# Layer 1 reads three of its four blocks from the buffers in which layer 0 left them

## The chip, the cores and the metric

The kernel runs on one core of a Trainium2 chip. That core has a tensor engine for matrix products (PE; its weight loads are shown as PEld), a vector engine (DVE), a scalar engine (ACT), GpSimd (POOL) and SyncE (SP), which here issues most of the transfers between the memory outside the core (DRAM) and the on-chip memory (SBUF). PE writes into a small second memory, PSUM, from which DVE and ACT read. Each engine runs its own list of instructions in order and waits at the head of it. The metric is the device time of one execution in microseconds (us).

## What is computed

Two layers over an input x of 2048 rows and 512 columns (f32). Each layer is a long convolution over the rows, one kernel of 2048 taps per column, and then a gated FFN with a hidden size of 1376. Both get a normalised x and add their result to x:

```
x = x + A(layernorm(x))      # y = causal convolution over the rows, + u * Dskip
x = x + B(layernorm(x))      # (silu(x @ w_gate) * (x @ w_up)) @ w_down
x = x + A(layernorm(x))      # layer 1: the same weights
x = x + B(layernorm(x))
```

## The kernel before

The rows are cut into four blocks of 512. A pair (layer, block) is a unit of work, and `SEQ` (line 43) lists the eight pairs in the order in which they are written: (0,0), (0,1), (0,2), (1,0), (0,3), (1,1), (1,2), (1,3). The convolution of a block works on spectra of 1024 points, in two halves h of 256 columns and four parts q. Block b multiplies the spectra of its own and of all b earlier blocks with those of the taps.

The steps of one unit, by name and line:

- `inputs` (713) loads the block's x into the tile `n` (`load_x`, 234), normalises it in place (`norm_x`, 252: ACT sums the rows into a scrap tile `junk` at 223 and 225, POOL and DVE make the factors at 227 and 228, ACT writes `n` at 255), and `forward` (259) transforms it: ACT and DVE split `n` into two f16 parts `z` (267, 268), PE multiplies at 277 into the PSUM tiles `pf`, ACT and DVE add and subtract into `fu` and `fbt` (278 to 293). POOL stores the spectra to DRAM (`udr`, 739). There is one buffer for `n`.
- `ssm_half` (749) loads earlier spectra `uu` and those of the taps `w` (808, 810), multiplies and adds on DVE (812, 815, 820, 821: seven of the instructions at 812 and 815 for each of the four parts of a half of block 3), and transforms back: ACT and DVE split into `yl` (776, 777), PE multiplies at 784 into the PSUM tiles `pi`, DVE adds `pi` to x in the block's buffer `xt` (`result`, 787; recorded at line 232). Before that, `load_x` at 830 brings x into `xt`.
- `pf` and `pi` take turns in two small PSUM buffers.
- `ffn_norm` (874) normalises `xt` once more, transposes it through DMA, and `ffn` (915) multiplies: `pgu` (930 to 933, two PSUM buffers), ACT and DVE make `sg`, `hh` and `hl` (936 to 939), `py` (946 to 948). At line 953 DVE adds `py` to `xt`. This is the unit's result. For layer 1 it is stored to `out` (955), for layer 0 to a DRAM tensor `xdr` with a place for every block (957).

There are three buffers for `xt`: `xs[0]` and `xs[1]` are halves of the tile `xg`, `xs[2]` is the tile `xf`. A unit takes buffer number (its place in `SEQ`) modulo 3: 0, 1, 2, 0, 1, 2, 0, 1. In layer 1 a unit loads its x from `xdr` twice, once into `n` and once into `xt`.

The loop at line 1263 writes, for each i, the convolution of unit i + 1 and then the FFN of unit i. `inputs` runs one part ahead: the first part of unit i + 2, with load and norm, is written with the last part of unit i + 1, so ahead of the FFN of unit i. Within this stage a planner puts each engine's instructions in order: from times that it reckons in advance, it takes the ready one of highest priority. The instructions in `tc.high_priority` (the products at 277 and 784, the FFN's norm, `sg`, `hh`, `hl` and the residual) go ahead of the others. All that comes before, up to about 330 us, is ordered by hand and isn't touched by the change.

Of the kernel before, what the change touches and what calls it, by code (L numbers as in the profile page):

```python
# [11 lines left out]
F32 = mybir.dt.float32  # L12
F16 = mybir.dt.float16
BF16 = mybir.dt.bfloat16
I32 = mybir.dt.int32
AF = mybir.ActivationFunctionType
# [5 lines left out]
L, D, F = 2048, 512, 1376  # L22
P = 128
T = 512
NB = L // T
# [15 lines left out]
INV = 2  # L41
LOW = [a for a in range(1, 33) if a % 2] + [8, 16, 24, 32]
SEQ = ((0, 0), (0, 1), (0, 2), (1, 0), (0, 3), (1, 1), (1, 2), (1, 3))


def dft_constants():
# [29 lines left out]
def kernel(ctx, tc, x, a_re, a_im, b_re, b_im, c_re, c_im, log_dt, d_skip,  # L76
                           w_gate, w_up, w_down, c_ef, c_ei, c_ek, c_am, c_eh, c_eih, out):
    nc = tc.nc
# [10 lines left out]
    def tl(shape, name, tag, dt=F32):  # L89
        return sb.tile(shape, dt, name=name, tag=tag, bufs=BUFS[tag])  # L90
# [59 lines left out]

    wdr = dram.tile([NB, 2, 4, P, NQ, 2, DC], F32, name="wdr")
    udr = [dram.tile([NB - 1, 2, 4, P, NQ, 2, DC], F32, name=f"udr{i}") for i in range(NL)]
    xdr = dram.tile([NB, 4, P, D], F32, name="xdr")
    kdr = dram.tile([2, 4, 32, 4, 256], F32, name="kdr")
    ndr = dram.tile([2, 2, P, 2, HD], F32, name="ndr")

# [74 lines left out]
    def stt(o, i0, s, i1, op1):  # L231
        V.scalar_tensor_tensor(o, i0, s, i1, OP.mult, op1)  # L232

    def load_x(xt, layer, b):
        if layer == 0:
            nc.sync.dma_start(xt, x[0, b * T:(b + 1) * T, :].rearrange("(p c) d -> p c d", p=P))
        else:
            nc.sync.dma_start(xt, xdr[b].rearrange("c p d -> p c d"))

    def parted(t):  # L240

# [7 lines left out]

        return t.rearrange("p i (c d) -> p i c d", c=NQ)  # L250

    def norm_x(n):
        rs, nb = row_stats(n, 4, 1.0, "stats", lambda r: tl([P, D], "junk", "t1", BF16))
        for c in range(4):
            A.activation(n[:, c], n[:, c], AF.Identity, scale=rs[:, c:c + 1], bias=nb[:, c:c + 1])

    fs, fss = [], []

# [454 lines left out]
    def inputs():  # L713

        for layer, b in SEQ:
            if layer == 0 and b < 2:
                if b == 0:
                    nc.sync.dma_start(u4, udr[0][0, 0].rearrange("q p c i d -> p q c i d"))
                for h in range(2):
                    for i, q in enumerate(QORD):  # L720
                        if b == 0:
                            u = u4[:, q]
                            for qn in (QORD[:3], QORD[3:], (), ())[i] if h else ():
                                nc.sync.dma_start(u4[:, qn], udr[0][0, 1, qn])
                        else:
                            u = tl([P, NQ, 2, DC], "u", "u")
                            nc.sync.dma_start(u, udr[0][b, h, q])
                        yield h, q, u
                continue
            n = tl([P, 4, D], "n", "n")  # L730
            load_x(n, layer, b)
            norm_x(n)
            if (layer, b) == SEQ[HALF]:
                eh.append(tl([P, 4, 2, 2, P], "eh", "ef", F16))
                nc.sync.dma_start(eh[0], c_eh)
            for h in range(2):
                for q, u in forward(n, h, eh[0]):
                    if b < NB - 1:
                        G.dma_start(udr[layer][b, h, q], spectrum(u))
                    yield h, q, u  # L740
# [8 lines left out]
    def ssm_half(layer, b, h):  # L749
        first = layer == 0 and b == 0  # L750
        half = SEQ.index((layer, b)) >= INV
        hs = slice(h * HD, (h + 1) * HD)
        free = iv[h] if first else iv[0]

        def slot():
            return free.pop(0) if free else tl([P, 2, HD], "yf", "w")

        def done(t):
            if any(t is o for o in ivs):
                free.append(t)  # L760
        if half and not yl2:
            yl2.append(tl([P, 2, 2, 2, HD], "yl2", "hf", F16))

        def add_sub(x, y):

            t = slot()
            V.tensor_tensor(t, x, y, OP.add)
            V.tensor_tensor(x, x, y, OP.subtract)
            done(y)
            return t, x  # L770

        def inverse(pi, r, v):

            if half:
                yl = yl2[0][:, r % 2]
                A.activation(yl[:, 0], v, AF.Copy, scale=sy[:, 0:1])
                stt(yl[:, 1], v, sy[:, 0:1], yl[:, 0], OP.subtract)
            with tc.high_priority(offset=0 if first else BOOST):
                if half:
                    terms = [(eih[:, r, i, le], yl[:, ly, i]) for i in range(2) for le, ly in ((0, 0), (0, 1), (1, 0))]  # L780
                else:
                    terms = [(ei[:, r, i], v[:, i]) for i in range(2)]
                for k, (e, o) in enumerate(terms):
                    PE.matmul(pi[:, r % 2], lhsT=e, rhs=o, start=k == 0, stop=k == len(terms) - 1)  # L784
            done(v)

        def result(pi, r):

            o = xt[:, r:r + 2, hs]
            if half:  # L790
                stt(o, pi, sy[:, 1:2], o, OP.add)
            else:
                V.tensor_tensor(o, o, pi, OP.add)

        xt = xs[SEQ.index((layer, b)) % 3]
        ys = []
        for s in range(4):
            hq, q, u = ahead.pop(0)
            nxt = next(spec, None)
            if nxt:  # L800
                ahead.append(nxt)
            yk = tl([P, NQ, 2, 2, DC], "yk", "y1")
            for k in range(b + 1):
                if k == 0:
                    w, uu = w0r[:, h, q], spectrum(u) if any(u is o for o in fss) else u
                else:
                    w = tl([P, NQ, 2, DC], "w", "w")
                    nc.sync.dma_start(w, wdr[k, h, q])
                    uu = tl([P, NQ, 2, DC], "uu", "uu")
                    nc.sync.dma_start(uu, udr[layer][b - k, h, q])  # L810
                t = tl([P, NQ, 2, 2, DC], "t", "t") if k else yk
                V.tensor_tensor(t, uu.unsqueeze(2).to_broadcast([P, NQ, 2, 2, DC]),  # L812
                                w.unsqueeze(3).to_broadcast([P, NQ, 2, 2, DC]), OP.mult)
                if k:
                    V.tensor_tensor(yk, yk, t, OP.add)  # L815
            if any(u is o for o in fss):
                fs.append(u)
            y = slot()
            yo = whole(y)
            V.tensor_tensor(yo[:, 0], yk[:, :, 0, 0], yk[:, :, 1, 1], OP.subtract)  # L820
            V.tensor_tensor(yo[:, 1], yk[:, :, 0, 1], yk[:, :, 1, 0], OP.add)
            if (layer, b, h, s) == (0, 1, 0, 0):
                yield
            ys.append(y)
            if s % 2:
                ys[s - 1:] = add_sub(*ys[s - 1:])
            if s == 3:
                a_, b_, c_, d_ = ys
                if h == 0 and not first:
                    load_x(xt, layer, b)  # L830
                pi = psml([P, 2, HD], "pi")
                v0 = slot()
                V.tensor_tensor(v0, a_, c_, OP.add)
                inverse(pi, 0, v0)
                v1 = slot()
                V.tensor_tensor(v1[:, 0], b_[:, 0], d_[:, 1], OP.subtract)
                V.tensor_tensor(v1[:, 1], b_[:, 1], d_[:, 0], OP.add)
                inverse(pi, 1, v1)
            yield
        pj = psml([P, 2, HD], "pi")  # L840
        V.tensor_tensor(a_, a_, c_, OP.subtract)
        done(c_)
        inverse(pj, 2, a_)
        V.tensor_tensor(b_[:, 0], b_[:, 0], d_[:, 1], OP.add)
        V.tensor_tensor(b_[:, 1], b_[:, 1], d_[:, 0], OP.subtract)
        done(d_)
        inverse(pj, 3, b_)
        result(pi, 0)
        yield
        result(pj, 2)  # L850
        yield
# [22 lines left out]
    def ffn_norm(layer, b, s):  # L874

        rows = TB // P
        xt = xs[SEQ.index((layer, b)) % 3][:, s * rows:(s + 1) * rows]
        nh, nlo = nhl2[:, s % 2, 0], nhl2[:, s % 2, 1]
        with tc.high_priority(offset=BOOST):
            rs, nb = row_stats(xt, rows, 256.0, "stats2", lambda r: nn2[:, r])  # L880
# [34 lines left out]
    def ffn(layer, b, ready=None):  # L915
        for s in range(T // TB):
            rows = TB // P
            xt = xs[SEQ.index((layer, b)) % 3][:, s * rows:(s + 1) * rows]
            nh, nlo = ready if ready and s == 0 else ffn_norm(layer, b, s)
            for f0 in (0, 2, 4, 6, FT - 1, 8) if ready and s == 0 else (FT - 1, 0, 2, 4, 6, 8):  # L920
                pgu = pbig([P, 2, 2, TB], "pgu")
# [21 lines left out]
            for r, f in steps if final else sorted(steps, key=lambda o: o[1]):  # L943
                rc = slice(r * P, (r + 1) * P)
                n = min(P, F - f * P)
# [6 lines left out]
                with tc.high_priority(offset=BOOST):  # L952
                    V.scalar_tensor_tensor(xt[:, r], py[r], sc6[:, 5:6], xt[:, r], OP.mult, OP.add)
                    if layer == NL - 1:
                        nc.sync.dma_start(out[0, b * T:(b + 1) * T, :].rearrange("(p c) d -> c p d", c=4)[c], xt[:, r])
                    else:
                        nc.sync.dma_start(xdr[b, c], xt[:, r])

    ts = [None] * (NCH + 2)
    gs = [None] * (NCH + 2)  # L960
# [346 lines left out]
```

## Time and profile before

| what | us |
|---|---|
| median of 3 runs (lowest to highest) | 1092.52 (1089.46 to 1093.47) |
| the profiled execution | 1091.58 |
| its span, first to last instruction | 1089.4 |
| PE busy / DVE busy / ACT busy | 1026.5 / 969.3 / 547.4 |
| mean granted clock of PE | 0.986 |

How the rows are read. A row of the timeline has the start in us from the span's start, the duration in us, the engine, the line, the operation, output <- inputs by the names of the program, shapes, a count, and in brackets how long the engine had stood idle and what ended that. A row of the waits has who waited, for whom, the total in us, how often, and the longest. A row of the stages has the window, its length, and for each engine the busy time and the number of instructions, then the granted clock, the share of time that the DMA engines worked, and GB/s. A row of the transfers has out<-in, the queue, the count, the KB of one and the median us from issue to landing. `xg` and `xf` stand for the buffers `xs`, `in_A_u_dram` for the input x.

### The profile page before, as it was taken

To read this page: it belongs to the slowest core of one execution; us is meant where nothing else is said; L and a number is where in the kernel's file an instruction comes from. 1 tells how busy PE (TensorE), PEld (TensorE's weight loads), DVE (VectorE), ACT (ScalarE), POOL (GpSimd) and SP (SyncE) were. 2 spreads that over 40 slices of the span, in tenths; PEclk is the share of its full clock that TensorE was granted. 3 is DMA by queue.
4 is the path that set the end of the run, shared out by engine and by line. 5 is a ranking of instruction groups with operands and counts; after the bars stand their busy time and mean duration, and the time that the engine had idled before them with its cause. 6 is when DMAs were issued, how large, how long until landed. Compare 5 with 4: busy or idle time off the path is not lost.

```text
span 1089.4 us, 22811 instructions
## 1 busy us (share of the span) xinstructions
PE 1026.5 (94%) x9302; PEld 810.9 (74%) x9302; DVE 969.3 (89%) x1405; ACT 547.4 (50%) x1093; POOL 109.6 (10%) x163
## 2 busy tenths in 40 slices
PE   1989999998779999999999999999999999999998
PEld 1868888887677777686779676786867687686775
DVE  8999999998999999999999989999998999993221
ACT  6989998953367162466462253533425432134211
POOL 1112222220002010012010001201100000000000
PEclk9989999998989999999999999999999999999999
DMA  5366777768765356342444553443545245312000
GB/s 212 108 180 167 173 166 179 187 181 272 234 182 172 120 145 215 105 141 68 131 117 133 158 160 130 119 136 100 166 126 180 59 127 147 109 61 63 2 25 20
DMA packets 125003, 149.23 MB, mean 137 GB/s; under 512 B 50897, under 2 KB 75985, under 8 KB 124130
## 3 DMA queue, kind: packets, MB, share of 16 engines
q1 hardware_dynamic: 112994, 122.27, 36.8%
q0 software_dynamic: 11904, 25.50, 10.0%
q8 instruction: 73, 1.20, 0.5%
q14 instruction: 32, 0.26, 0.1%
HBM read 97.66 MB, written 33.82 MB: 121 GB/s over the span
## 4 chain that ended last, share of the span: by engine, by line
PE 27%; DVE 27%; issue 11%; DMA 5%; ACT 3%; POOL 1%; SPq 0%; DVEq 0%; POOLq 0%; ACTq 0%
PE pgu L930 5%; PE pgu L931 5%; PE pgu L933 5%; DVE t L812 4%; DVE yk L815 4%; PE py L948 3%; PE py L946 3%; PE py L947 3%; DVE yk L812 3%; PE pi L784 2%; DVE sg L937 2%; DVE hl L939 2%; DMA n<-xdr 1%; DVE yl L232 1%; DMA mix<-nn 1%
## 5 line engine op out<-in xcount | busy, mean ns | idle before, releaser
L930 PE MATMUL pgu<-mix,wsl 128*128 128x256 f16 x1280 | 298.6, 273 | 5.4 <-DVE sg L937 2.1
L931 PE MATMUL pgu<-mix,wsl 128*128 128x256 f16 x1280 | 298.4, 273 | 0.0
L933 PE MATMUL pgu<-mix,wsl 128*128 128x256 f16 x1280 | 194.8, 273 | 0.0
L931 PEld LDWEIGHTS <-wsl 128*128 128x128 f16 x1280 | 125.2, 98 | 22.5 <-issue 6.7
L933 PEld LDWEIGHTS <-wsl 128*128 128x128 f16 x1280 | 125.2, 98 | 18.4 <-issue 3.8
L930 PEld LDWEIGHTS <-wsl 128*128 128x128 f16 x1280 | 125.2, 98 | 16.4 <-issue 1.2
L946 PE MATMUL py<-wsl,hh 128*128 128x512 f16 (+1 forms) x352 | 134.2, 381 | 0.1
L948 PE MATMUL py<-wsl,hl 128*128 128x512 f16 (+1 forms) x352 | 133.5, 381 | 0.1
L947 PE MATMUL py<-wsl,hh 128*128 128x512 f16 x320 | 121.8, 381 | 0.0
L815 DVE TENSOR_TENSOR yk<-yk,t 128x1024 f32<-128x1024 f32 x96 | 116.9, 1218 | 0.5
L812 DVE TENSOR_TENSOR t<-uu,w 128x1024 f32<-128x1024 f32 x96 | 117.0, 1218 | 0.3
L938 ACT ACTIVATE hh<-sg 128x512 f16<-128x512 f32 x80 | 50.1, 627 | 114.0 <-DVE sg L937 114.0
L544 PE MATMUL pw<-kt,ek 128*128 128x256 f32 (+1 forms) x384 | 93.2, 381 | 0.0
L937 DVE SCALAR_TENSOR_TENSOR sg<-pgu,sc,sg 128x512 f32<-128x512 f32 x80 | 59.6, 745 | 37.7 <-ACT sg L936 37.6
L936 ACT ACTIVATE sg<-pgu,sc 128x512 f32<-128x512 f32 x80 | 54.2, 678 | 70.7 <-PE pgu L933 66.9
L544 PEld LDWEIGHTS pw<-kt,ek 128*128 128x128 f32 x384 | 74.8, 199 | 8.8
L939 DVE TENSOR_TENSOR hl<-sg,hh 128x512 f16<-128x512 f32 x80 | 54.8, 685 | 15.3 <-ACT hh L938 15.3
L227 POOL TENSOR_TENSOR rs<-mv,mhalf 128x2 f32<-128x2 f32 (+1 forms) x21 | 33.6, 1598 | 336.3 <-ACT mv L226 296.3
L509 PE MATMUL pk<-re,g 128*32 128x64 f32 x1024 | 65.0, 317 | 2.2 <-DMA g<-g 1.9
L948 PEld LDWEIGHTS <-hl 128*128 128x128 f16 (+1 forms) x352 | 34.4, 98 | 39.2 <-issue 0.8
L947 PEld LDWEIGHTS <-hh 128*128 128x128 f16 (+1 forms) x352 | 34.6, 98 | 38.4 <-issue 0.8
L510 PE MATMUL pk<-im,g 128*32 128x64 f32 x1024 | 63.1, 301 | 0.0
(265 smaller groups left out, 2010.1 us busy)
## 6 DMA issues: line engine op xcount, KB each, us to landing
uu<-udr SPq DMA_DIRECT2D x96, 256.0 KB, 3.0
w<-wdr SPq DMA_DIRECT2D x96, 256.0 KB, 2.8
g<-g POOLq DMA_DIRECT2D x6, 1024.0 KB, 9.2
udr<-fu POOLq DMA_DIRECT2D x22, 256.0 KB, 2.7
udr<-u SPq DMA_DIRECT2D x16, 256.0 KB, 3.3
n<-xdr SPq DMA_DIRECT2D x4, 1024.0 KB, 6.4
kdr<-ks SPq DMA_DIRECT2D x6, 512.0 KB, 2.9
kt<-kdr SPq DMA_DIRECT2D x24, 128.0 KB, 3.0
```

Of the source, the lines that this page charges most:

```text
L509: PE.matmul(o, lhsT=g[:, 0, :, d], rhs=re[:, 0:64, d], start=True, stop=False, tile_position=(0, 32 * grp))
L544: PE.matmul(pw[:, i], lhsT=e, rhs=kt[:, :, c + 4 * k0:4 * k1:4, :].rearrange("p g k d -> p k g d"), start=c == 0, stop=c == 3)
L812: V.tensor_tensor(t, uu.unsqueeze(2).to_broadcast([P, NQ, 2, 2, DC]), w.unsqueeze(3).to_broadcast([P, NQ, 2, 2, DC]), OP.mult)
L815: V.tensor_tensor(yk, yk, t, OP.add)
L930: PE.matmul(o, lhsT=wgu(wi, k, 0)[:, fs], rhs=nh[:, k], start=k == 0, stop=False)
L931: PE.matmul(o, lhsT=wgu(wi, k, 1)[:, fs], rhs=nh[:, k], start=False, stop=False)
L933: PE.matmul(o, lhsT=wgu(wi, k, 0)[:, fs], rhs=nlo[:, k], start=False, stop=k == 3)
L937: V.scalar_tensor_tensor(sg, pgu[:, 1], sc6[:, 4:5], sg, OP.mult, OP.mult)
L939: V.tensor_tensor(hl[:, f0:f0 + 2], sg, hh[:, f0:f0 + 2], OP.subtract)
L946: PE.matmul(py[r], lhsT=hh[:n, f, rc], rhs=wd(f, 0)[:n], start=f == 0, stop=False)
L947: PE.matmul(py[r], lhsT=hh[:n, f, rc], rhs=wd(f, 1)[:n], start=False, stop=False)
L948: PE.matmul(py[r], lhsT=hl[:n, f, rc], rhs=wd(f, 0)[:n], start=False, stop=f == FT - 1)
```

## The change

The buffers are given out by a table, `HOME`, in place of the count modulo 3. Blocks 0, 1 and 3 have the same buffer in both layers (0, 1 and 2); block 2 has buffer 2 in layer 0 and buffer 0 in layer 1. Between the layers only block 2 goes through `xdr`, which shrinks to one block. For the other three, `norm_x` in layer 1 reads the block's buffer and writes `n`, and the convolution's result is added where x already lies.

```diff
+HOME = (0, 1, 2, 0, 2, 1, 0, 2)
+MOVED = 2
...
-    xdr = dram.tile([NB, 4, P, D], F32, name="xdr")
+    xdr = dram.tile([4, P, D], F32, name="xdr")
...
+    def moved(layer, b):
+        return layer == 0 or b == MOVED
+
...
-            nc.sync.dma_start(xt, xdr[b].rearrange("c p d -> p c d"))
+            nc.sync.dma_start(xt, xdr.rearrange("c p d -> p c d"))
...
-    def norm_x(n):
-        rs, nb = row_stats(n, 4, 1.0, "stats", lambda r: tl([P, D], "junk", "t1", BF16))
+    def norm_x(n, xt):
+        rs, nb = row_stats(xt, 4, 1.0, "stats", lambda r: tl([P, D], "junk", "t1", BF16))
         for c in range(4):
-            A.activation(n[:, c], n[:, c], AF.Identity, scale=rs[:, c:c + 1], bias=nb[:, c:c + 1])
+            A.activation(n[:, c], xt[:, c], AF.Identity, scale=rs[:, c:c + 1], bias=nb[:, c:c + 1])
...
             n = tl([P, 4, D], "n", "n")
-            load_x(n, layer, b)
-            norm_x(n)
+            xt = n if moved(layer, b) else xs[HOME[SEQ.index((layer, b))]]
+            if xt is n:
+                load_x(n, layer, b)
+            norm_x(n, xt)
...
-        xt = xs[SEQ.index((layer, b)) % 3]
+        xt = xs[HOME[SEQ.index((layer, b))]]
...
-                if h == 0 and not first:
+                if h == 0 and not first and moved(layer, b):
                     load_x(xt, layer, b)
...
-                    else:
-                        nc.sync.dma_start(xdr[b, c], xt[:, r])
+                    elif moved(1, b):
+                        nc.sync.dma_start(xdr[c], xt[:, r])
```

`ffn_norm` and `ffn` take their buffer from `HOME` in the same way. The unit (0,3) thereby has buffer 2 instead of buffer 1, so its x is loaded into the buffer that the unit (0,2) leaves.

More of the change, by code (lines that the diff above doesn't have):

```diff
@@ L876, in ffn_norm @@
         rows = TB // P
-        xt = xs[SEQ.index((layer, b)) % 3][:, s * rows:(s + 1) * rows]
+        xt = xs[HOME[SEQ.index((layer, b))]][:, s * rows:(s + 1) * rows]
         nh, nlo = nhl2[:, s % 2, 0], nhl2[:, s % 2, 1]
@@ L917, in ffn @@
             rows = TB // P
-            xt = xs[SEQ.index((layer, b)) % 3][:, s * rows:(s + 1) * rows]
+            xt = xs[HOME[SEQ.index((layer, b))]][:, s * rows:(s + 1) * rows]
             nh, nlo = ready if ready and s == 0 else ffn_norm(layer, b, s)
```

## The prediction

> **What bounds the kernel now.** I read the page first: the busy times of the engines.
>
> ```profile
> span 1089.4 us, 22811 instructions
> PE 1026.5 (94%) x9302; PEld 810.9 (74%) x9302; DVE 969.3 (89%) x1405; ACT 547.4 (50%) x1093; POOL 109.6 (10%) x163
> ```
>
> Two engines look full, so an average decides nothing. Next the view of stages. From 390 us on the kernel does what the change touches: the blocks after the first ones, conv of one block beside the FFN of another.
>
> ```profile
> core 0: us, PE busy (x) PEld busy (x) DVE busy (x) ACT busy (x) POOL busy (x), PEclk, DMA share, GB/s
> 390.00:920.00 530.00, 517.51 (x4314) 392.90 (x4312) 510.18 (x756) 230.87 (x451) 40.97 (x55) 1.00 0.45 133
> 920.00:1000.00 80.00, 80.00 (x636) 59.36 (x634) 63.65 (x89) 29.72 (x54) 1.80 (x4) 1.00 0.25 72
> 1000.00:1089.00 89.00, 85.20 (x710) 63.87 (x707) 20.91 (x31) 14.74 (x24) 0.20 (x1) 1.00 0.08 25
> ```
>
> Up to 920 us both PE (517.51 of 530) and DVE (510.18) are full. In the last 169 us DVE works 63.65 + 20.91 = 84.56 us and PE 165.2. So conv is done early and PE carries on alone at a granted clock of 1.00: the end is set by PE's work plus the time PE stands still. The matmuls aren't changed. What can be won is PE's idle time, which is 12.49 us before 920. The view of waits, PE alone, from 390 us on, says for whom it stood:
>
> ```profile
> PE pi L784 <- ACT yl L776: 5.8, 4, 2.0
> PE pf L277 <- ACT fbt L278: 2.5, 1, 2.5
> PE pgu L930 <- DVE sg L937: 2.1, 2, 1.6
> PE pf L277 <- ACT z L267: 1.0, 1, 1.0
> PE pi L784 <- DVE yl L232: 0.3, 1, 0.3
> ```
>
> That is 11.7 us in nine waits, the ceiling of any gain: 1091.58 - 11.7 = 1079.9 us. Six of the nine end with ACT, although ACT is only 230.87 of 530 us busy. ACT isn't slow, it is held: its queue runs in order.
>
> **What the change removes.** Loads and stores of x between the layers:
>
> ```profile
> n<-xdr SPq DMA_DIRECT2D x4, 1024.0 KB, 6.4
> xg<-xdr SPq DMA_DIRECT2D x3, 1024.0 KB, 8.0
> xf<-xdr SPq DMA_DIRECT2D x1, 1024.0 KB, 5.6
> xdr<-xg SPq DMA_DIRECT2D x12, 256.0 KB, 3.9
> ```
>
> Of these (and of four more stores, xdr<-xf) only block 2's remain: three loads into n, three into xs and 12 stores go, 9 MB. With DMA at a share of 0.45, the bytes themselves are worth nothing: no wait of PE above names a transfer.
>
> The loads into xs lie hidden too: DVE's adds at line 789 need them, and no wait names them. They go for nothing.
>
> The loads into n are not hidden. In the timeline, ACT's first instruction on a loaded n is the head of ACT's queue, and what stands behind it is late. ACT first, then the PE rows that follow:
>
> ```profile
> 433.08 0.63 ACT L223 ACTIVATE junk<-n 128x512 bf16<-128x512 f32 x1 [2.74 <-DMA n<-xdr]
> 536.14 0.63 ACT L223 ACTIVATE junk<-n 128x512 bf16<-128x512 f32 x1 [3.51 <-DMA n<-xdr]
> 638.30 0.63 ACT L223 ACTIVATE junk<-n 128x512 bf16<-128x512 f32 x1 [4.55 <-DMA n<-xdr]
> 825.03 0.63 ACT L223 ACTIVATE junk<-n 128x512 bf16<-128x512 f32 x1 [5.30 <-DMA n<-xdr]
> ...
> 436.30 0.27 PE L784 MATMUL pi<-yl,mix 128*128 128x256 f16 x1 [1.41 <-ACT yl L776]
> 539.33 0.27 PE L784 MATMUL pi<-yl,mix 128*128 128x256 f16 x1 [2.02 <-ACT yl L776]
> 633.14 0.27 PE L930 MATMUL pgu<-mix,wsl 128*128 128x256 f16 x1 [1.64 <-DVE sg L937]
> 837.63 0.38 PE L277 MATMUL pf<-z,eh 128*128 128x256 f16 x2 [0.99 <-ACT z L267]
> ```
>
> The four ACT rows are blocks 0, 1, 2 and 3 of layer 1. Block 2 keeps its load. For block 1, say: ACT stands from 532.6 to 536.14, runs its norm, and yl gets its turn only then; PE idles 2.02 us for it. The three loads that go account for 1.41 + 2.02 + 0.99 = **4.42 us** of PE's idle time.
>
> When will the data be there instead? When the FFN's residual (line 953) has written it:
>
> ```profile
> 418.67 0.75 DVE L953 SCALAR_TENSOR_TENSOR xg<-py,sc,xg 128x512 f32<-128x512 f32 x1
> 520.29 1.40 DVE L953 SCALAR_TENSOR_TENSOR xg<-py,sc,xg 128x512 f32<-128x512 f32 x2
> 813.65 0.74 DVE L953 SCALAR_TENSOR_TENSOR xg<-py,sc,xg 128x512 f32<-128x512 f32 x1
> ```
>
> Those end at 419.42, 521.69 and 814.39, so the norm may begin 13.7, 14.5 and 10.6 us earlier than it does. ACT's instructions are the same in number and shape, so they cost what they cost; the last four, which write n, still wait until n's former reader is done. What is late next is PSUM and DVE: pf shares two small buffers with pi, so an early norm doesn't bring pf forward by as much. I therefore count the PE waits named, and no more.
>
> SyncE also stands at the head of its own queue for the stores:
>
> ```profile
> SPq L238 <- DMA xdr<-xg: 4.1, 1, 4.1
> SPq L238 <- DMA xdr<-xf: 2.1, 1, 2.1
> ```
>
> The first (block 3) goes. The second (block 1's load into xs, at 620.76 below) goes, but a load for block 3 of layer 0 stands there instead with the same wait. Behind them are loads of w and uu, which no DVE wait names: nothing.
>
> **What it adds.** Block 3 of layer 0 moves from the buffer of block 1 to that of block 2, whose FFN ends just before. Its load and its first adds now, beside that FFN's end:
>
> ```profile
> 524.02 0.33 SPq L236 DMA_DIRECT2D xg<-in_A_u_dram  x1
> ...
> 612.64 0.74 DVE L232 SCALAR_TENSOR_TENSOR xg<-pi,sy,xg 128x512 f32<-128x512 f32 x1
> 616.90 1.40 DVE L953 SCALAR_TENSOR_TENSOR xf<-py,sc,xf 128x512 f32<-128x512 f32 x2
> 619.35 0.75 DVE L232 SCALAR_TENSOR_TENSOR xg<-pi,sy,xg 128x512 f32<-128x512 f32 x1
> 620.76 0.37 SPq L238 DMA_DIRECT2D xf<-xdr  x1
> ```
>
> Before, the load is issued 88 us ahead of its use. After, it needs the residual of block 2 (ends 618.30) and the store of it. That is the condition of the xf<-xdr load at 620.76, and it lands 5.6 us later, at 626.4. So the adds of block 3's first half, now at 612.64 and 619.35, can't run before 626.4. Their place in DVE's queue is at the earliest behind the residual that they depend on, at 618.3, so DVE can stand 626.4 - 618.3 = 8.1 us at most for this landing. Behind it in the queue would be block 3's products of the second half, sg and hl of the FFN, and so PE's next pgu.
>
> The trace has no such wait on DVE, so I bound it. How much other work is at hand there, the stage says, and how long the products behind it are, the group of line 812:
>
> ```profile
> 612.00:627.00 15.00, 15.00 (x156) 12.33 (x154) 14.97 (x20) 3.25 (x6) 0.00 (x0) 1.00 0.63 215
> ```
> ```profile
> L812 DVE TENSOR_TENSOR t<-uu,w 128x1024 f32<-128x1024 f32 x96 | 117.0, 1218 | 0.3
> ```
>
> Of DVE's 14.97 us the two adds are 1.5 and the residual 1.4, so 12 us are other work. The cost is nothing if the order puts that first; a gain I exclude, as the load starts 97 us later than now. Its other end is 8.1 us, and 628.8 - 618.3 = 10.5 us if the landing takes the 8.0 us of xg<-xdr. The nearest row is block 2's wait: a load of the same 1 MB at the same place, 4.55 us on ACT and **1.64 us** on PE. I take that. The two PSUM buffers of pi are held some 7 to 14 us longer as well; pf of the next block follows later. But ahead of that block's products stand those of block 3's second half, four parts of seven such instructions, 4 x 7 x 1.218 = 34 us, so I count nothing.
>
> **Sum**, against the profiled execution's own time of 1091.58 us (span 1089.4 and 2.2 around it; 0.9 below the median of 1092.52): 1091.58 - 4.42 + 1.64 = **1088.8 us**.
>
> **Rivals.**
>
> *The reused buffer holds DVE (slower).* Place: the add into xs[2] right behind line 953, near 618 us. Price: up to 10.5 us of DVE, which PE feels as soon as both pgu buffers wait for sg. It decides if the products aren't put ahead of the add. For it: DVE is full up to 920, so nothing is caught up there; the orders before are optimistic about loads, as all four ACT rows show. Against: the 12 us of other work at hand. Uncovered, and the three waits of PE back in the shifted order behind it: 1091.58 + 8.1 = 1099.7. With those gains kept: 1087.16 + 8.1 = 1095.3, and 1097.7 with the longer landing.
>
> The Trainium skill (Trainium Kernel Development and Optimization, section Best Practices) advises double-buffering so that DMA overlaps with compute, and here a rotation of three is given up at one place. By that rule the sum is this rival's. The load at 524.02, 88 us ahead of its use, is what the rule asks for, and the trace agrees that no add waited for it.
>
> *Nothing changes (1091.6).* PE's waits come from the order in which pi and pf are put ahead of pgu, not from the loads, and return elsewhere when the order is made anew. For it, PE waits with none of these loads just ahead of them, in PE's timeline:
>
> ```profile
> 476.53 0.27 PE L784 MATMUL pi<-yl,mix 128*128 128x256 f16 x1 [0.99 <-ACT yl L776]
> 665.30 0.27 PE L784 MATMUL pi<-yl,mix 128*128 128x256 f16 x1 [1.40 <-ACT yl L776]
> 868.32 0.81 PE L277 MATMUL pf<-z,eh 128*128 128x256 f16 x6 [2.50 <-ACT fbt L278]
> ```
>
> Against: three waits follow directly on the loads that go.
>
> *The earlier norms cure more (faster).* Ten to 14 us of slack ahead of pf and of block 3's conv take away all PE waits but block 2's (1.64) and the one of 0.99: 11.7 - 2.6 = 9.1, so 1082.5. For it: the 2.50 us on fbt fall in block 3's forward transform, 43 us behind its late norm at 825.03. Against: pf waits for PSUM.
>
> **Chances.** Forecast, 1085 to 1091: 0.36, of which 0.06 lies beyond 0.5% (5.5 us, about what a measurement of this kernel can tell from no change). Faster rival: 0.26. No change: 0.14. The held DVE: 0.24, of which 0.06 stays within 0.5%. So faster 0.06 + 0.26 = 0.32, same 0.30 + 0.14 + 0.06 = 0.50, slower 0.18. The range runs from 1081, just under the faster rival, to 1100, at the held DVE's uncovered price; left out are the ceiling of 1079.9 and both prices of the held DVE at once.
>
> **What would show it.** Right: no ACT row junk<-xs with a DMA as releaser for blocks 0, 1 and 3; the PE waits on yl at blocks 0 and 1 gone; PE's idle time in 390 to 920 down from 12.49 to some 9.7 us; block 2's load still with an ACT wait of 3 to 5 us. The reused buffer shows as a DVE wait on xf<-in_A_u_dram: under 3 us fits, 8 us is the rival. Wrong would be: PE idle unchanged with the loads gone (waits are made by the order), or conv work reaching past 1000 us so that PE no longer ends alone.

## The result, and the profile after

The changed kernel takes 1085.02 us (median of 5 runs, 1082.94 to 1087.11) against 1092.52 us (1089.46 to 1093.47): a ratio of 0.994, 95% interval 0.9918 to 0.9961. That is 0.6% faster. The profiled execution took 1085.02 us with a span of 1082.8.

The view of the stages of the changed kernel, with the columns of before (window, length, then busy time and count of PE, PEld, DVE, ACT, POOL):

```profile
390.00:920.00 530.00, 522.52 (x4382) 399.21 (x4380) 518.77 (x769) 233.51 (x452) 42.49 (x55) 1.00 0.40 118
920.00:1000.00 80.00, 80.00 (x664) 59.51 (x663) 57.82 (x81) 26.87 (x52) 2.05 (x4) 1.00 0.28 76
1000.00:1083.00 83.00, 78.52 (x620) 57.73 (x617) 18.11 (x26) 13.96 (x22) 0.20 (x1) 0.99 0.05 16
```

PE's idle time up to 920 us is 530 - 522.52 = 7.48 us; it was 12.49. After 920 us PE again works on alone while DVE runs dry. So the end is still PE's work plus PE's pauses. PE's waits in the same stretch:

```profile
PE pgu L937 <- DVE sg L915: 3.0, 3, 1.8
PE pi L791 <- ACT yl L783: 1.6, 1, 1.6
PE pgu L937 <- DVE sg L944: 1.4, 2, 1.1
PE pf L282 <- DVE xg L234: 0.9, 1, 0.9
PE pf L282 <- DVE xf L234: 0.4, 1, 0.4
```

They are 7.3 us in eight waits, against 11.7 in nine. But the list isn't the old one less three rows. The waits on yl at 436 and 539 us are gone, as are the one at 633 and those on pf behind ACT (837 and 868 us); waits on sg (line 915 was 908) and on the adds (line 234) are new. From the first residual to the last, the view of the residual's line gives 371.3 to 1085.2 us before and 372.1 to 1078.6 after, 713.9 and 706.5 us. Of the 7.4 us between them 4.9 are idle time of PE. The other 2.5 us are busy time on the same 5811 matmuls (701.4 us before, 698.9 after), and they aren't shown to come from the change: up to 330 us, which none of the changes here touches, `late_load` and `split_x` below have PE busy for 285.44 and 282.27 us, for 3145 matmuls each.

ACT's waits ahead of the norm, in the view of ACT's waits (the third row is unit (0,3), the others are layer 1):

```profile
ACT junk L225 <- DVE xg L960: 13.7, 4, 7.2
ACT junk L225 <- DVE xf L960: 7.3, 1, 7.3
ACT junk L225 <- DMA n<-in_A_u_dram: 3.8, 1, 3.8
ACT junk L225 <- DMA n<-xdr: 2.0, 1, 2.0
```

For the three blocks the releaser is now the residual on DVE, where it was a transfer. ACT begins these norms 14.6 to 16.1 us earlier (at 417.46, 520.05 and 810.46 us), but it waits no less: 13.7 + 7.3 + 2.0 = 23.0 us for layer 1, against 16.1 us for the loads before.

The price that the prediction feared, on DVE and on SyncE:

```profile
614.75 1.41 DVE L960 SCALAR_TENSOR_TENSOR xf<-py,sc,xf 128x512 f32<-128x512 f32 x2
...
623.22 1.41 DVE L234 SCALAR_TENSOR_TENSOR xf<-pi,sy,xf 128x512 f32<-128x512 f32 x2 [0.55 <-DMA xf<-in_A_u_dram]
```
```profile
618.27 0.33 SPq L241 DMA_DIRECT2D xf<-in_A_u_dram  x1
```

The load for (0,3) starts at 618.27, as reckoned, and the adds come 10.6 and 4.5 us later than they did. DVE waits 0.55 us for it. The planner had put seven other instructions between the residual and the adds.

The time lies at the low end of the forecast, 1085 to 1091. The experiments show that the reason given for it was not the cause.

### The profile page after: what moved, and what is told of

Its sections match the earlier page's. It is cut to its first block, busy times and chain, and to the rows that moved or that the text cites. A ratio compares the mean times of both kernels' runs of the same rounds, so it can differ in the third digit from the quotient of the medians.

```text
span 1082.8 us, 22772 instructions
## 1 busy us (share of the span) xinstructions
PE 1022.1 (94%) x9302; PEld 808.7 (75%) x9302; DVE 968.5 (89%) x1405; ACT 547.5 (51%) x1093; POOL 110.3 (10%) x163
## 4 chain that ended last, share of the span: by engine, by line
DVE 34%; PE 23%; issue 8%; DMA 5%; ACT 2%; POOL 2%; SPq 0%; DVEq 0%; ACTq 0%; POOLq 0%
DVE t L819 6%; DVE yk L822 5%; PE pgu L937 5%; PE pgu L938 5%; PE pgu L940 5%; DVE yk L819 3%; DVE sg L944 2%; PE py L953 2%; PE py L955 2%; PE py L954 2%; DVE hl L946 2%; DMA mix<-nn 2%; POOL rs L229 2%; DVE yl L234 2%; PE pi L791 1%
## 5 line engine op out<-in xcount | busy, mean ns | idle before, releaser
L937 PEld LDWEIGHTS <-wsl 128*128 128x128 f16 x1280 | 125.2, 98 | 15.4 <-issue 0.2
```

The lines of the kernel that those rows point to most:

```text
L937: PE.matmul(o, lhsT=wgu(wi, k, 0)[:, fs], rhs=nh[:, k], start=k == 0, stop=False)
```

## Experiments

Their ratios are against runs of the kernel before on the same chip, whose medians were 1091.9, 1091.85 and 1091.56 us in the three sets. PE's idle time below is 530 less PE's busy time in 390 to 920 us.

### The loads put back

`order_only` gives out the buffers in the new order and loads everything as before:

```diff
-    def moved(layer, b):
-        return layer == 0 or b == MOVED
+    def moved(layer, b, kept):
+        return layer == 0 or b not in kept
...
+NDIRECT = ()      # blocks whose norm reads the buffer
+XDIRECT = ()      # blocks that are not loaded into it again
```

> Buffers in the new order, but every block of layer 1 loads x from DRAM twice as before. Theory A (the loads into n, waited for at the head of ACT's queue, cost PE its idle time): the four ACT waits on n<-xdr are back with 2 to 5 us each, PE idle from the first residual to the last is near the 12.5 us of before, and the time is 1091 to 1094. Theory B (the new order of the buffers and the order of instructions planned from it bring the gain): near 1085. Theory C (the late load of block 3 in layer 0 costs something that the gain outweighs): 1 to 3 us above the kernel before.

`n_load_back` has `NDIRECT = ()` and `XDIRECT = (0, 1, 3)`.

> As the changed kernel, but blocks 0, 1 and 3 of layer 1 are stored and loaded into n again; nothing is loaded into xs for them. Theory A: the ACT waits on n<-xdr are back, 1089 to 1094. Theory B: 1085. Theory D (the loads into xs and what they do to SyncE's queue are what cost): 1085 to 1087, although ACT waits.

`xs_load_back` has `NDIRECT = (0, 1, 3)` and `XDIRECT = ()`.

> As the changed kernel, with n written straight from the buffers, but the three blocks are stored and loaded once more into the buffer in which they already lie. Theory A: no ACT wait on n<-xdr for blocks 0, 1 and 3, 1084 to 1087. Theory D: 1088 to 1092.

`old_order_b0` has the old order of buffers, and both sets are `(0,)`.

> The kernel before, with its own order of buffers (block 0 has buffer 0 in both layers there), where block 0 alone is read straight from its buffer. Theory A: the first of the four ACT waits goes and with it the PE wait of 1.41 us near 436 us; 1.4 to 2.5 us below the kernel before, 1090 to 1091. Theory B: no change, 1092 to 1093.

| run | median us | ratio, interval | PE idle us |
|---|---|---|---|
| order_only | 1085.18 | 0.9937 (0.9919 to 0.9956) | 8.80 |
| n_load_back | 1083.83 | 0.9921 (0.9901 to 0.9942) | 6.62 |
| xs_load_back | 1083.65 | 0.9925 (0.9907 to 0.9944) | 8.79 |
| old_order_b0 | 1091.71 | 1.0003 (0.9988 to 1.0017) | 14.15 |

Theory A falls with `order_only` and `n_load_back`: with the loads into n back the whole gain stays. In `old_order_b0`, with the loads and stores of block 0 gone and the old order, no gain is left. `xs_load_back` alone would fit theory A, whose 1084 to 1087 it meets but for 0.4 us. Theory C (the late load costs something) falls with `order_only`, which is faster than the kernel before. The views of ACT's and of PE's waits in `order_only`:

```profile
ACT junk L226 <- DMA n<-xdr: 12.4, 4, 3.9
```
```profile
PE pi L792 <- ACT yl L784: 4.7, 3, 2.4
PE pgu L938 <- DVE sg L945: 1.7, 2, 1.1
PE py L954 <- ACT hh L946: 1.1, 1, 1.1
PE pgu L938 <- DVE sg L916: 0.5, 1, 0.5
PE py L956 <- DVE hl L947: 0.3, 1, 0.3
```

ACT waits 12.4 us for the four loads (16.1 before), and PE's waits on yl are there as well, with those near 436 and 539 us among them. What is missing are PE's waits on pf behind ACT. So those didn't hang on the loads. Those near 436 and 539 us did: each is there in every run of this document that loads that block into n, and in none that reads it from the buffer. But where both are gone, as in the changed kernel, four new pauses on sg and on the adds stand between 472 and 535 us, 3.2 us in all. In `old_order_b0` the wait at 436 us did go, as theory A says, and 5.11 us near 648 us came:

```profile
648.22 0.27 PE L938 MATMUL pgu<-mix,wsl 128*128 128x256 f16 x1 [5.11 <-DVE sg L945]
```
```profile
640.92 0.63 ACT L226 ACTIVATE junk<-n 128x512 bf16<-128x512 f32 x1 [7.62 <-DMA n<-xdr]
```

ACT stands 7.62 us there for block 2's n, a load that the changed kernel keeps too, and the FFN's `hh` and `sg` come behind it. So a load into n can cost PE time; the gain just isn't made of that. Theory D (the loads into the buffers cost) falls with `xs_load_back` and `order_only`, which have these loads and are fast. What is left is the order of the buffers.

### Which part of the new order

The new order changes little: (0,3) follows (0,2) in a buffer and so is loaded late, (1,1) follows (0,1) and could be loaded early. The next four have all loads of the kernel before, except as said.

`late_load`, old order of buffers:

```diff
+                    if (layer, b) == (0, 3):
+                        nc.sync.dma_start(xt[:, 0, 0:1], xs[2][:, 3, 0:1])
                     load_x(xt, layer, b)
```

> The kernel before, buffers in the old order and all loads as before, but the load of x for (0,3) is held back by a transfer of one element per row that reads block 2's buffer after its FFN: it starts near 620 us instead of 524, as in the changed kernel. Theory B2 (the late load makes the planner put the adds of (0,3) behind the products of its second half, and that order is the better one): 1084 to 1087. Theory B1 (the load for (1,1) at 621 us is what costs in the old order): 1092 to 1095.

`no_load_11` has the old order and `XDIRECT = (1,)`.

> The kernel before with the load of x into the buffer of (1,1) left out (block 1 of layer 1 then adds to what block 2 left there); its load into n stays. Theory B1: 1084 to 1087. Theory B2: 1090 to 1093.

`home_a` has `HOME = (0, 1, 2, 0, 2, 1, 0, 1)`.

> All loads as before; (0,3) has buffer 2 and (1,1) buffer 1 as in the changed kernel, but (1,3) takes buffer 1 after (1,1) instead of buffer 2 after (0,3), so its load into the buffer comes only near 912 us. B1 and B2 both say 1084 to 1088, as what they name is unchanged. Theory B3 (no one dependency decides, each plan draws its own waits): anywhere from 1083 to 1094.

`home_b` has `HOME = (0, 1, 2, 0, 1, 2, 0, 2)`.

> All loads as before; (0,3) has buffer 1 and (1,1) buffer 2 as in the kernel before, but (1,3) takes buffer 2 after (1,1). B1 and B2: 1090 to 1094. B3: anywhere from 1083 to 1094.

| run | median us | ratio, interval | PE idle us |
|---|---|---|---|
| late_load | 1084.25 | 0.9932 (0.9906 to 0.9959) | 7.37 |
| no_load_11 | 1092.34 | 1.0 (0.9987 to 1.0013) | 14.36 |
| home_a | 1087.57 | 0.9966 (0.9948 to 0.9984) | 7.19 |
| home_b | 1092.5 | 0.9997 (0.9983 to 1.0011) | 11.26 |

`late_load` is the kernel before with one load held back, plus one small transfer, and it has the whole gain. Its load and its adds:

```profile
619.20 0.34 SPq L242 DMA_DIRECT2D xg<-in_A_u_dram  x1
```
```profile
624.07 1.41 DVE L235 SCALAR_TENSOR_TENSOR xg<-pi,sy,xg 128x512 f32<-128x512 f32 x2 [0.95 <-DMA xg<-in_A_u_dram]
```

DVE waits 0.95 us that it didn't wait before, and the kernel is 0.7% faster. B1 falls with `no_load_11`, which leaves out the load that B1 blames and is no faster. `home_a` and `home_b` came out as B2 says, which B3 allows too. `home_a` keeps most of the gain; it also has one new wait of PE on yl, beyond the stretch that the table counts:

```profile
922.08 0.27 PE L792 MATMUL pi<-yl,mix 128*128 128x256 f16 x1 [1.67 <-ACT yl L784]
```

The four kernels so far with the old time (before, `old_order_b0`, `no_load_11`, `home_b`) have three pauses of PE in common, here from the PE waits of `home_b`:

```profile
PE pgu L938 <- DVE sg L945: 3.1, 1, 3.1
PE pf L283 <- ACT fbt L284: 2.2, 1, 2.2
PE pf L283 <- ACT z L273: 1.0, 1, 1.0
```

All four have the wait on fbt (2.2 to 2.5 us, near 868), on z (1.0, near 837) and one on sg soon after block 2's residual: 1.64 us at 633 before, 3.11 at 633 in `no_load_11`, 3.08 at 635 in `home_b`, and the 5.11 at 648 in `old_order_b0`. No other kernel here has any of the three (`split_x` below has one of 0.7 us on fbt, but near 759). They come to 5.1 to 8.5 us, and the idle time that is left without them, 5.0 to 8.1 us, is like that of the fast kernels. How the one on fbt comes about shows in ACT's timeline of the kernel before:

```profile
863.53 0.82 ACT L883 ACTIVATE nn<-xg,rs 128x512 f32<-128x512 f32 x1 [1.75 <-DVE nn L885]
867.15 0.63 ACT L884 ACTIVATE nn<-nn 128x512 f16<-128x512 f32 x1 [2.81 <-DMA mix<-nn]
867.69 0.58 ACT L278 ACTIVATE fbt<-pf 128x512 f32<-128x512 f32 x1
```

and in that of `order_only`:

```profile
865.45 0.81 ACT L891 ACTIVATE nn<-xg,rs 128x512 f32<-128x512 f32 x1
866.15 0.58 ACT L284 ACTIVATE fbt<-pf 128x512 f32<-128x512 f32 x1
...
869.33 0.63 ACT L892 ACTIVATE nn<-nn 128x512 f16<-128x512 f32 x1 [0.94 <-DMA mix<-nn]
```

The same three instructions: before, the copy fbt stands behind one that waits 2.81 us for a transpose of the FFN's norm; in the other order it stands ahead of it. That transpose isn't a load of x at all. Here the order of ACT's queue decides whether PE waits, some 245 us after the load that was held back.

The pause at 633 us lies close behind that load. DVE's rows of the kernel before, then those of the changed one:

```profile
629.47 1.22 DVE L232 SCALAR_TENSOR_TENSOR z<-n,z 128x1024 f16<-128x1024 f32 x1
632.34 0.74 DVE L937 SCALAR_TENSOR_TENSOR sg<-pgu,sc,sg 128x512 f32<-128x512 f32 x1
```
```profile
626.35 0.75 DVE L944 SCALAR_TENSOR_TENSOR sg<-pgu,sc,sg 128x512 f32<-128x512 f32 x1
636.41 1.23 DVE L234 SCALAR_TENSOR_TENSOR z<-n,z 128x1024 f16<-128x1024 f32 x1
```

In the old order DVE runs z, and the adds into `fbt` and `fu` with it, ahead of the FFN's sg for which PE stands; in the new one sg comes first. They belong to the forward transform of (1,1). From the start of block 2's residual to that of sg it is 15.4 us before (616.90 to 632.34), in `no_load_11` and in `home_b`, and 9 to 12 us in all other kernels here. (In `old_order_b0`, one of those, the pause comes from ACT's wait of 7.62 us instead.)

### What about the late load does it

`late_adds`, old order, load at 524 us:

```diff
                     load_x(xt, layer, b)
+                    if (layer, b) == (0, 3):
+                        for r in (0, 2):
+                            nc.sync.dma_start(xt[:, r, 0:1], xs[2][:, 3, 0:1])
+                            nc.sync.dma_start(xt[:, r, 0:1], x[0, b * T:(b + 1) * T, :].rearrange("(p c) d -> p c d", p=P)[:, r, 0:1])
```

> The kernel before; the load of x for (0,3) stays at 524 us, but the adds into it are held back: two single elements per row are overwritten from block 2's buffer after its FFN and then loaded again from x. If it is the adds of (0,3) and what they release that had to come late: 1083 to 1087, as with the late load. If it is the transfer of 1 MB at 524 us that cost (beside the load into n for (1,1)): 1090 to 1093.

`late_forward`, old order, adds not touched:

```diff
+            if (layer, b) == (1, 1):
+                nc.sync.dma_start(eh[0][:, 0, 0, 0, 0:2].bitcast(F32), xs[2][:, 3, 0:1])
+                nc.sync.dma_start(eh[0][:, 0, 0, 0, 0:2], c_eh[:, 0, 0, 0, 0:2])
             for h in range(2):
                 for q, u in forward(n, h, eh[0]):
```

> The kernel before; the adds of (0,3) stay early, but the forward transform of (1,1) is held back until after block 2's FFN, by one element of its matrix that is overwritten from block 2's buffer and loaded again. If the late adds help by keeping the two small PSUM buffers, so that pf of (1,1) and with it the load into n and the norm of (1,2) come later: 1084 to 1087. If they help by their place in DVE's own order: 1090 to 1093.

`split_x`, the changed kernel with `load_x` in parts:

```diff
+        src = x[0, b * T:(b + 1) * T, :].rearrange("(p c) d -> p c d", p=P) if layer == 0 else xdr.rearrange("c p d -> p c d")
+        k = 4 // parts
+        for c in range(0, 4, k):
+            nc.sync.dma_start(xt[:, c:c + k], src[:, c:c + k])
...
-                    load_x(xt, layer, b)
+                    load_x(xt, layer, b, 2)
```

> The changed kernel with the loads of x into the buffers cut in two halves of the rows. The first half for (0,3) then needs only the first half of block 2's FFN (573 us), so one of the two adds comes early again, near 612 us. If both adds must be late: back towards 1089 to 1092. If the second one alone keeps PSUM long enough: 1084 to 1086. A reader of DVE's wait alone (0.6 us on this load) would say 1084.

`split_n` has the same `load_x`, with `load_x(n, layer, b, 4)` alone.

> The changed kernel with every load into n that remains (blocks 2 and 3 of layer 0, block 2 of layer 1) cut into four of 256 KB, so that ACT's norm may start on the first quarter. If ACT's waits on n cost PE nothing, as the runs with the loads back say: 1084 to 1086. If they cost what stands in the waits (3.8 and 2.0 us on ACT): 1082 to 1084, the best of all.

| run | median us | ratio, interval | PE idle us |
|---|---|---|---|
| late_adds | 1090.32 | 0.9987 (0.997 to 1.0004) | 10.70 |
| late_forward | 1085.26 | 0.994 (0.9916 to 0.9964) | 6.88 |
| split_x | 1083.38 | 0.992 (0.9892 to 0.9948) | 5.97 |
| split_n | 1086.85 | 0.9953 (0.9935 to 0.997) | 8.12 |

By its expectation `late_adds` would put the cost on the 1 MB transfer at 524 us. But `late_forward` has that transfer at the same place, 524.43 us, and is fast. The gain comes without late adds too: in `late_forward` they run at 613.23 and 619.95 us, and it is as fast as the changed kernel. Only the forward transform of (1,1) is held there. So B2, which named the adds, falls as it was put. ACT's split z, a part of that transform, first in the kernel before, then in `late_forward`:

```profile
626.08 1.06 ACT L267 ACTIVATE z<-n 128x1024 f16<-128x1024 f32 x1 [2.90 <-PE pf L277]
```
```profile
631.55 1.06 ACT L273 ACTIVATE z<-n 128x1024 f16<-128x1024 f32 x1 [1.75 <-PE pf L283]
```

That spoke for the two PSUM buffers of pi as the link. The other two runs don't bear it out as a rule. In `late_adds` adds and z are late (622.27 and 630.97 us), PE's waits at 837 and 868 us are gone, and others have come:

```profile
PE pi L792 <- ACT yl L784: 7.5, 3, 3.0
PE pgu L942 <- DVE sg L949: 2.9, 2, 1.7
PE py L960 <- DVE hl L951: 0.3, 1, 0.3
```

It has four more transfers than the kernel before, of which two wait; what these cost wasn't measured by itself. In `split_x` the first add is early again and z is not late, while the median is the lowest of all:

```profile
608.91 0.74 DVE L234 SCALAR_TENSOR_TENSOR xf<-pi,sy,xf 128x512 f32<-128x512 f32 x1
...
620.67 0.74 DVE L234 SCALAR_TENSOR_TENSOR xf<-pi,sy,xf 128x512 f32<-128x512 f32 x1
```
```profile
622.75 1.06 ACT L272 ACTIVATE z<-n 128x1024 f16<-128x1024 f32 x1 [0.57 <-PE pf L282]
```

`split_n` doesn't do what it was meant to:

```profile
ACT junk L225 <- DMA n<-in_A_u_dram: 6.8, 2, 4.9
ACT junk L225 <- DMA n<-xdr: 5.6, 3, 5.0
```

ACT begins the norm of (0,3) 2.8 us and that of block 2 0.6 us sooner than in the changed kernel, but it now waits for single quarters as well, 12.4 us in all against 5.8. The time lies outside both expectations, and the run decides nothing. `split_x` is 1.6 us below the changed kernel by the medians, but their intervals against the kernel before overlap widely, so it isn't shown to be better.

**What is shown:** no load of x that the change removes carries the gain. The place in time of (0,3)'s load, or of the forward transform behind it, is enough for all of it in the old kernel. The orders of DVE's and ACT's instructions differ from there on, and the three pauses of PE that the slow orders share are gone. **What stays open:** whether one rule makes those orders better, or each plan draws its own pauses (B3). Late adds and a late z are neither both needed (`late_forward`, `split_x`) nor enough (`late_adds`). `late_adds` is without the three pauses as well, and others cost it nearly as much. Each order has pauses of its own, and no run here holds the order fixed while a single wait is taken away.

## Why the prediction came out, and where it was wrong

- **The bound was right.** PE's work plus PE's pauses sets the end. PE's idle time in 390 to 920 us follows the times: 11.3 to 14.4 us in the four slow kernels, 6 to 8.8 in those below 1088, 10.7 in `late_adds`. The ceiling of 1079.9 us wasn't reached.
- **"The three loads that go account for 4.42 us": this step failed.** A wait of ACT on n does stand just ahead of the two pauses on yl; the third, 0.99 us, begins 11.6 us after ACT's wait is over. But with the loads back (`order_only`) ACT's waits and the two pauses on yl were back and the time was not, and without the first load in the old order the first pause went and 5.11 us came elsewhere. A pause next to a wait isn't its price when all orders are planned anew.
- **"4.55 us on ACT and 1.64 us on PE": these two rows were misread.** PE's pause ends at 633.14 us, and ACT's wait for block 2's n begins only at 638.30 - 4.55 = 633.75. So that load can't have caused it, and the + 1.64 us of the sum has no row behind it. The pause is the one in which sg stood behind z on DVE, and it is gone with the late load.
- **"A gain I exclude, as the load starts 97 us later than now": this failed too, and it is the larger error.** The late load was entered at + 1.64 us. By itself it is worth 1091.85 - 1084.25 = 7.6 us of gain (4.5 to 10 by the interval). Its direct cost was in the range given, 0.55 us of DVE's wait. What the sum lacked was that a new dependency also moves everything that the planner places after it.
- **That the time fell into the forecast is luck.** The sum had 2.8 us of gain from two terms that don't hold; the profiled executions are 6.6 us apart and the medians 7.5. Nor could the signs named tell: the transfers went from ACT's rows, both pauses on yl went, PE's idle time fell (to 7.48 us, not 9.7), and DVE waited under 3 us. All that came with a gain that the loads didn't make. One sign failed: block 2's load cost ACT 2.0 us, not 3 to 5.
- **The rival in which the reused buffer holds DVE** did not come about: DVE's wait was 0.55 us and not 8.1, since the planner put other work first, as was held against it. The Trainium skill's advice (Trainium Kernel Development and Optimization, section Best Practices) to double-buffer so that DMA overlaps with compute speaks against a load as late as this one; the runs differ, as the kernel with the late load is the faster one.
- **The rival "nothing changes"** had the better mechanism: the sum of the pauses comes from the order and not from the loads. Its time was wrong, as it took it that a new order brings back as much as it takes away. Here it took away more, and alike in five kernels with quite different loads.
- **The rival of earlier norms** came nearest by the time (1082.5), but not by its cause: `n_load_back` has none of the earlier norms and runs at 1083.83 us.
- The loads into the buffers, the 9 MB and SyncE's waits were entered at nothing, which `order_only`, `n_load_back` and `xs_load_back` bear out.

## What to carry to other kernels

Where a planner makes the order, test a change of loads or buffers first with its dependencies alone and its work left as it was: here that gave the whole gain, and what the change was named for gave none that could be measured. A wait that stands next to a pause of the bounding engine is a suspect, and its price is known only when it is taken away. Here a load that starts some 95 us later made the kernel faster, and what changed with it is which instructions come first on DVE and ACT.

## What the runs showed of the hardware

An engine that has little to do can hold the one that bounds the kernel: ACT, busy 230.87 of 530 us, kept PE waiting 2.5 us by a copy of 0.58 us that stood behind an instruction waiting 2.81 us for a transpose. Beyond that the chip behaved as the first trace had it; the surprise was in the order of the instructions.
